# Seven half products for the output of blocks 3 to 8, made transposed from sums of w_out

## The chip, the core and the metric

The kernel runs on one core of a Trainium2 chip. The metric is device time in microseconds (us) of one execution, the median of several runs. A core has five engines that work beside one another and wait for each other by semaphores: TensorE (PE; its weight loads are shown as PEld), VectorE (DVE), ScalarE (ACT), GpSimd (POOL) and SyncE (SP), whose queue here issues nearly all transfers. Every engine executes its own instructions in the order in which they were listed.

## The reference

Attention with 8 batches, 8 heads, 576 positions of 64 dimensions; heads 0 to 3 see the last 32 positions, heads 4 to 7 see positions whose index has the same remainder by 32. Its result, 4608 tokens of 512 numbers, goes through a gated layer of 1536 hidden columns. All of it is in float32.

```python
scores = np.where(masks, scale * q @ k.T, -1e9)          # per batch and head
attn = softmax(scores); x = (attn @ v) laid out as (4608, 512)
gate = 1.0 / (1.0 + np.exp(-(x @ w_gate)))               # (4608, 1536)
val = x @ w_val
out = (gate * val @ w_out).astype(np.float32)            # (4608, 512)
```

## The kernel before

**Precision.** A float32 operand is split into a high part and a rest in the type F32R. Every product is made of three matmuls: high with high, high with low, low with high. So "three" below is always this.

**Tiling.** Tokens are worked on in nine blocks of 512: blocks 0 to 7 are the first 512 positions of each batch, block 8 holds the 64 left-over positions of each. The hidden columns are 12 slices of 128 (f), the 512 input columns are four chunks of 128.

**Blocks 0 to 2** are plain: for each f a gate product (`g`) and a val product (`v`) of 12 matmuls each, ScalarE's sigmoid (`s`), VectorE's product (`m`), the hidden tile's high part by ScalarE (`x`) and low part by VectorE (`y`), then 12 matmuls of the output (`o`: hidden tile stationary, w_out moving, four token tiles of 128 x 512 in two pairs of PSUM banks).

**Blocks 3 to 8** go in three super-blocks of two blocks (k = 3, 5, 7 is the first). Gate and val of two blocks by a pair of slices (q = 0 to 5) are a product of 2 x 2 block matrices, and are made by seven products of half the work in place of eight: `G` (gate) and `V` (val), six matmuls each, for the products p = 1, 2, 6, 5, 7, 4, 3. The moving side are seven sets of sums and differences of x (`xd`, then high parts `xh` by ScalarE and low parts `xl` by VectorE). The stationary side are sums of weights. GpSimd makes them (`pa`, `pb`), ScalarE and VectorE split them (`ph`, `pw`), and they are stored (`pd`; plain ones `pl`) in device memory as `sets`. They come back through a ring of five slots for six sets, 512 KB a set (`r`). PSUM sums of several products are combined by ScalarE's copies (`c`), VectorE's additions (`ad`), ScalarE's sigmoid (`sg`) and VectorE's products (`mu`). The result are the hidden tiles of four quarters: two blocks by two slices.

The output products of blocks 3 to 8 are those of blocks 0 to 2, `o`, 12 matmuls for each block and f: block k's stand between the sets of its own super-block, block k+1's behind them. I call the 42 sets of a super-block its product stage and what follows its output stage.

**Attention** of batches 2 to 7 runs in 24 pieces (n = 0 to 23, four for each block; 12 to 19 are blocks 5 and 6), spread between the products: queries and values are loaded (`LQ`, `LV`), scores (`S`) and values (`X`) are short matmuls, which stand together and which I call an interlude; VectorE has mask, maximum, subtraction, sum, reciprocal, normalization (`M`, `A`, `U`, `N`, `W`) and eight 32-row transposes (`B`), ScalarE the exponential (`E`). The pieces of a super-block have to be done before its sets of x are made.

**Order.** The text `ORDER` lists all steps one by one; each step's instructions are issued to their engines' queues at that place, and no scheduler moves them. SyncE's queue is in the same order: a ring load stands in it behind stores that wait for VectorE and loads that wait for a buffer.

Names of tiles in the rows: `p` and `d` are PSUM accumulators of `G` and `V`, `xs` the sets of x, `ring` a ring slot, `o` (also `o_a`, `o_g`, `o_v`) output accumulators, `hid`, `h`, `e` hidden tiles and what they are made from, `hh`, `hl` the two parts, `sb`, `mx`, `pt` the attention's, `sum`, `sumh` the weight sums.

Of the kernel before, what the change touches and what calls it, by code (L numbers as in the profile page):

```python
# [20 lines left out]
DM, DF = 512, 1536  # L21
# [40 lines left out]
USE = "1265743"  # L62

# [121 lines left out]


@with_exitstack
def attention_then_glu(ctx, tc, qk_l, qk_s, v_l, v_s, w_all, consts, out):
# [11 lines left out]
    def left_over(b):  # L200
# [5 lines left out]
        if b == 6:  # L206
            xr[6] = stage("h0", "xr6").bitcast(F32).rearrange("p (c n) -> p c n", c=NC)
# [423 lines left out]
    def give_out(k, i, cut=slice(0, DM), by=None):  # L631
# [8 lines left out]
        if k < B:  # L640
            return
# [426 lines left out]
```

## Time and profile before

| | |
|---|---|
| runs | 927.53, 928.52, 930.17 us; median 928.52 |
| span of the profiled execution (the page gives it no other time) | 927.6 us |
| TensorE busy | 919.8 us, 99% |
| VectorE busy | 599.9 us, 65% |
| ScalarE busy | 426.8 us, 46% |
| GpSimd busy | 179.9 us, 19% |
| moved by the DMA queues | 154.19 MB, 166 GB/s |

The span runs from the first to the last instruction. An engine's share is a mean over the whole span; stages differ. A row of a group has the line, the engine, the operation, out<-in, the count, the busy time in us, the mean length of one in ns, and the idle time before it. Matmuls are pipelined: the length of one is longer than the distance to the next.

### The profile page before, as it was taken

To read this page: it belongs to the slowest core of one execution; us is meant where nothing else is said; L and a number is where in the kernel's file an instruction comes from. 1 tells how busy PE (TensorE), PEld (TensorE's weight loads), DVE (VectorE), ACT (ScalarE), POOL (GpSimd) and SP (SyncE) were. 2 spreads that over 40 slices of the span, in tenths; PEclk is the share of its full clock that TensorE was granted. 3 is DMA by queue.
4 is the path that set the end of the run, shared out by engine and by line. 5 is a ranking of instruction groups with operands and counts; after the bars stand their busy time and mean duration, and the time that the engine had idled before them with its cause. 6 is when DMAs were issued, how large, how long until landed. Compare 5 with 4: busy or idle time off the path is not lost.

```text
span 927.6 us, 18516 instructions
## 1 busy us (share of the span) xinstructions
PE 919.8 (99%) x7606; PEld 754.9 (81%) x7606; DVE 599.9 (65%) x959; ACT 426.8 (46%) x776; POOL 179.9 (19%) x243
## 2 busy tenths in 40 slices
PE   8999999999999999999999999999999999999998
PEld 5788888888888888888888888888888888888886
DVE  5898877667799899665667896766248333333331
ACT  5888754334546455443435544444335233332222
POOL 4452641554555321000000210000003000000000
PEclk9899999999999999999999999999999999999999
DMA  9862644465677455655645436654443055444111
GB/s 345 333 220 85 197 152 153 159 192 159 199 240 247 115 187 191 208 189 181 193 157 181 149 109 195 198 181 148 138 156 125 23 174 178 145 150 146 59 45 46
DMA packets 90195, 154.19 MB, mean 166 GB/s; under 512 B 5888, under 2 KB 40192, under 8 KB 90112
## 3 DMA queue, kind: packets, MB, share of 16 engines
q1 hardware_dynamic: 89712, 152.36, 50.9%
q8 instruction: 60, 0.98, 0.4%
q10 hardware_dynamic: 400, 0.66, 0.3%
q14 instruction: 23, 0.19, 0.1%
HBM read 121.53 MB, written 31.46 MB: 165 GB/s over the span
## 4 chain that ended last, share of the span: by engine, by line
PE 98%; ACT 1%; DVE 1%; issue 0%; POOL 0%; DVEq 0%; ACTq 0%; POOLq 0%
PE o L623 22%; PE p L887 21%; PE d L887 16%; PE g L592 10%; PE v L592 10%; PE o_a L623 5%; PE o_g L623 3%; PE o_v L623 3%; PE x_a L513 2%; PE x L513 1%; PE s_g L371 1%; PE s_v L371 1%; PE gv L592 1%; PE s L371 1%; PE unread L730 0%; ACT sb L435 0%
## 5 line engine op out<-in xcount | busy, mean ns | idle before, releaser
L887 PE MATMUL p<-xs,ring 128*128 128x512 f32 x864 | 204.6, 389 | 0.0
L887 PEld LDWEIGHTS p<-xs,ring 128*128 128x128 f32 x864 | 162.2, 188 | 33.7
L623 PE MATMUL o<-w,hh 128*128 128x512 f32 x576 | 180.6, 395 | 0.0
L887 PE MATMUL d<-xs,ring 128*128 128x512 f32 x648 | 155.6, 389 | 0.0
L887 PEld LDWEIGHTS d<-xs,ring 128*128 128x128 f32 x648 | 121.6, 188 | 25.2
L623 PEld LDWEIGHTS o<-w,hh 128*128 128x128 f32 x576 | 106.1, 188 | 22.7
L480 DVE STREAM_TRANSPOSE pt<-sb 32x320 f32<-32x320 f32 (+1 forms) x224 | 120.1, 536 | 4.5
L623 PE MATMUL o<-w,hl 128*128 128x512 f32 x288 | 112.0, 389 | 0.0
L921 DVE TENSOR_TENSOR e<-e,d 128x512 f32<-128x512 f32 x54 | 37.1, 687 | 110.6 <-PE d L887 62.5
L592 PE MATMUL g<-xh,w 128*128 128x512 f32 x256 | 85.9, 393 | 0.0
L916 ACT COPY e<-p 128x512 f32<-128x512 f32 x54 | 31.7, 587 | 116.8 <-PE p L887 116.8
L592 PE MATMUL v<-xh,w 128*128 128x512 f32 x256 | 85.2, 390 | 0.0
L623 PEld LDWEIGHTS o<-w,hl 128*128 128x128 f32 x288 | 54.1, 188 | 11.5
L592 PEld LDWEIGHTS g<-xh,w 128*128 128x128 f32 x256 | 48.5, 189 | 10.3
L592 PEld LDWEIGHTS v<-xh,w 128*128 128x128 f32 x256 | 48.0, 188 | 10.0
L815 POOL TENSOR_TENSOR sum<-sum 128x128 f32<-128x128 f32 x96 | 51.5, 540 | 6.3
L592 PE MATMUL g<-xl,w 128*128 128x512 f32 x128 | 50.3, 393 | 0.3 <-DVE xl L553 0.3
L616 DVE TENSOR_TENSOR hl<-hid,hh 128x512 fp32r<-128x512 f32 x36 | 28.0, 780 | 34.5 <-ACT hh L612 34.3
L592 PE MATMUL v<-xl,w 128*128 128x512 f32 x128 | 49.8, 389 | 0.0
L810 POOL TENSOR_TENSOR sum<-w 128x256 f32<-128x256 f32 x44 | 35.5, 827 | 72.7 <-DMA sets<-sum 49.4
L929 ACT ACTIVATE e<-e 128x512 f32<-128x512 f32 x54 | 34.2, 633 | 29.9 <-DVE e L921 29.9
L612 ACT CAST hh<-hid 128x512 fp32r<-128x512 f32 x36 | 22.4, 622 | 49.9 <-PE o_a L623 41.1
(164 smaller groups left out, 1416.6 us busy)
## 6 DMA issues: line engine op xcount, KB each, us to landing
ring<-sets SPq DMA_DIRECT2D x126, 512.0 KB, 4.1
raw<-in_w_all SPq DMA_DIRECT2D x36, 512.0 KB, 5.8
vv<-in_v_l SPq DMA_DIRECT2D x15, 640.0 KB, 4.6
qk<-in_qk_l SPq DMA_DIRECT2D x14, 608.0 KB, 5.2
qk<-in_qk_s SPq DMA_DIRECT2D x14, 594.0 KB, 6.0
out<-ob SPq DMA_DIRECT2D x32, 256.0 KB, 2.0
sets<-w SPq DMA_DIRECT2D x24, 256.0 KB, 3.3
sets<-sumh SPq DMA_DIRECT2D x24, 256.0 KB, 2.8
```

Source lines behind the costliest of these rows:

```text
L371: nc.tensor.matmul(sc[j % len(sc)][g * m : (g + 1) * m, j // len(sc) * BANK + (s - lo) * kk : j // len(sc) * BANK + (s - lo + 1) * kk], q[ ...
L480: nc.vector.transpose(dst[to : to + LB, :, col : col + LB], src[part * LB : (part + 1) * LB, :, h * LB : (h + 1) * LB])
L513: nc.tensor.matmul(at_bank(r, (u * per + g) * m, (u * per + g + 1) * m)[j * D : (j + 1) * D], v[part][rows, slot * P + j * D : slot * P + ...
L592: nc.tensor.matmul(o, w, x, start=first and n == 0, stop=last and n == len(todo) - 1)
L616: by.tensor_tensor(hl, whole_h.pop((k, f)), hh.bitcast(F32), op=ALU.subtract)
L623: nc.tensor.matmul(acc[k][i], h[:, i * P : (i + 1) * P], w, start=f == 0 and n == 0, stop=f == NF - 1 and n == 2,)
L810: nc.gpsimd.tensor_tensor(u[:, at : at + 2], part(wh[f][i], c), part(wl[f][i], c), op=ALU.add)
L815: nc.gpsimd.tensor_tensor(u[:, to], u[:, x], u[:, y], op=op)
L887: nc.tensor.matmul(to, w[:, (wi * 2 + c) * P : (wi * 2 + c + 1) * P], x[xi][:, c], start=p in (1, 2, 5) and c == j == 0, stop=c == 1 and j ...
L916: nc.scalar.copy(x, two[m, 0])
L921: nc.vector.tensor_tensor(x, x, two[m, 1], op=ALU.add)
L929: nc.scalar.activation(x, x, AF.Sigmoid)
```

## The change

The output of a super-block is also made by seven half products. Its result is transposed: 128 columns of the output by 512 tokens, accumulated over all 12 slices. Stationary are w_out's four quarters (by pair of slices and half of the columns) and four sums of them, moving are the hidden tiles and sums of them.

- Sums of w_out: `pa`, `pb`, `ph`, `pw`, `pd` get a third index (i = 2): 12 more of each step, listed from the end of block 2 on through the first product stage; plain quarters are stored by `po` in block 2. They lie in `osets`.
- The ring serves them too: 63 units more, 21 for each super-block behind its 42 sets, one unit for a product and four slices.
- A pair of slices keeps five hidden tiles (`hidden_tile`), in the room that w_out and late weights leave. GpSimd makes the sums in place (`ta`, `tb`, `tc`, `td`).
- An operand is split when its product comes: `hx` (ScalarE, high part), `hy` (VectorE, low part), in five pairs of tiles used in turn. `Oa`, `Ob` are three matmuls each, for the two column tiles. They follow the super-block's 42 sets, product by product, six pairs of slices each.
- Two accumulators for each column tile are used alternately; results are kept by ScalarE (`ok`), added to by VectorE (`oa`) and stored transposed (`os`). A second output holds them; the host only puts the pieces in place.
- The steps from the last third of block 2 on are listed anew. Attention pieces 18 and 19 now stand in the first product stage. Attention matmuls there use the banks that the output accumulators had.

```diff
+HIDDEN = ["w7_0", "w7_1", "w8_0", "w8_1"] + [f"w{f}_2" for f in range(LATE)]
+KEPT = {"1": 0, "2": 1, "6": 0, "5": 4, "7": 2, "4": 1, "3": 3}
+USE_OUT = "1265734"
 ORDER = """
-... G3.5.3 mu3.5.4 x3.11 V3.5.3 ad3.5.0.3 y3.11 sg3.5.3 o3.9 r39 ad3.5.1.3 mu3.5.3 xd5.0.0 X17.0 x4.0 xh5.0.5 y4.0 ...
+... V3.5.3 ad3.5.0.3 sg3.5.3 Oa3.0.1 ad3.5.1.3 r39 xh5.0.3 Oa3.1.1 mu3.5.3 Ob3.0.1 xl5.0.3 ta3.5 Oa3.2.1 hx3.5.1 Ob3.1.1 ...
+    def plain_out_sets(q):
+        to = out_set(q)
+        for n, w in ((0, wh), (1, wl)):
+            a, b = (w[f][2].bitcast(F32).rearrange("p (k c m) -> p k c m", k=2, c=2) for f in (2 * q, 2 * q + 1))
+            nc.sync.dma_start(to[:, 0, n], a[:, 0])
+            nc.sync.dma_start(to[:, 1:3, n], b)
...
-    duos = [(k, q, p) for k in SUPER for q in range(PAIRS) for p in USE]
+    units = []
+    for k in SUPER:
+        units += [(k, q, p) for q in range(PAIRS) for p in USE] + [(k, p, u) for p in USE_OUT for u in range(PAIRS // 2)]
...
+    def hidden_tile(k, q, n):
+        at = 5 * q + n
+        if (k, at // 2) not in hidden:
+            hidden[k, at // 2] = pool.tile([P, 2, TB], F32, tag=HIDDEN[at // 2], name=f"hid{k}_{at // 2}")
+        return hidden[k, at // 2][:, at % 2]
...
+    def out_sum(which):
+        def step(k, q, by=nc.gpsimd):
+            h = [hidden_tile(k, q, n) for n in range(5)]
+            to, x, y = {"a": (4, 2, 0), "b": (2, 3, 2), "c": (0, 3, 4), "d": (1, 1, 0)}[which]
+            by.tensor_tensor(h[to], h[x], h[y], op=ALU.subtract)
...
+    def out_high(k, q, p):
+        u = USE_OUT.index(str(p)) * PAIRS + q
+        if u % 5 < 3:
+            ops[q, p] = [work.tile([P, TB], F32R, tag=f"{n}{u % 5}", name=f"{n}{k}_{q}_{p}") for n in ("hh", "hl")]
+        else:
...
+            ops[q, p] = [op_room[k][:, u % 5 * 2 - 6 + n] for n in range(2)]
+        nc.scalar.copy(ops[q, p][0], hidden_tile(k, q, KEPT[str(p)]))
+
+    def out_low(k, q, p, by=nc.vector):
+        hh, hl = ops[q, p]
+        by.tensor_tensor(hl, hidden_tile(k, q, KEPT[str(p)]), hh.bitcast(F32), op=ALU.subtract)
+
+    def out_half(k, q, p, ms=(0, 1)):
+        w, x = ring[k, str(p), q], ops[q, p]
+        at = int(p in (2, 5, 3))
+        for m in ms:
...
+            for j, (wi, xi) in enumerate(((0, 0), (0, 1), (1, 0))):
+                nc.tensor.matmul(
+                    chains[m, at],
+                    w[:, (wi * 2 + m) * P : (wi * 2 + m + 1) * P],
+                    x[xi],
...
+    def out_store(k, m, p):
+        i, j = {2: (0, 0), 7: (1, 1), 4: (1, 0), 3: (0, 1)}[p]
+        at = (k - SUPER[0] + j) * TB
+        nc.sync.dma_start(out_t[(2 * i + m) * P : (2 * i + m + 1) * P, at : at + TB], out_got[m, {2: 1, 7: 5, 3: 6, 4: 4}[p]])
```

TensorE's instructions at the end of the first product stage, before: `d` is the last set's accumulator, `o` an output step of block 3, `x_a` the values of attention piece 17.

```order
L887 MATMUL d_5_5842<-xs_3_1_4146,ring_5831 128x512
L887 MATMUL d_5_5842<-xs_3_0_4120,ring_5831 128x512
L623 MATMUL o_0_4689<-w_2_1424,hh_9_5688 128x512 x2
L623 MATMUL o_0_4689<-w_2_1424,hl_9_5689 128x512
L623 MATMUL o_0_4689<-w_2_1424,hh_9_5688 128x512 x2
L623 MATMUL o_0_4689<-w_2_1424,hl_9_5689 128x512
L623 MATMUL o_1_4690<-w_2_1424,hh_9_5688 128x512 x2
```

And after: `oc` is an accumulator of the new output products, `hh` and `hl` the operand of a pair of slices.

```order
L930 MATMUL d_5_6056<-xs_3_1_4174,ring_6047 128x512
L930 MATMUL d_5_6056<-xs_3_0_4153,ring_6047 128x512
L1009 MATMUL oc_0_1_6172<-hh_0_1_4686,ring_6074 128x512
L1009 MATMUL oc_0_1_6172<-hl_0_1_4687,ring_6074 128x512
L1009 MATMUL oc_0_1_6172<-hh_0_1_4686,ring_6074 128x512
L1009 MATMUL oc_0_1_6172<-hh_1_1_4923,ring_6074 128x512
L1009 MATMUL oc_0_1_6172<-hl_1_1_4924,ring_6074 128x512
```

The stationary side of the output now comes from the ring, which runs on without a pause; three matmuls belong to one pair of slices, and no output matmul is left inside the product stage.

VectorE's instructions for the third pair of slices in that stage, before: L390 to L459 and L480 are attention, L921 the sums of PSUM accumulators, L938 gate times val, L616 the low part of a hidden tile.

```order
L459 TENSOR_TENSOR sb_2_5033<-sb_2_5033,mx_2_5034 128x640
L480 STREAM_TRANSPOSE pt_2_5072<-sb_2_5033 32x10x32 x2
L921 TENSOR_TENSOR e_2_1_5058<-e_2_1_5058,d_2_5061 128x512
L480 STREAM_TRANSPOSE pt_2_5072<-sb_2_5033 32x10x32 x2
L921 TENSOR_TENSOR h_2_5070<-h_2_5070,d_2_5075 128x512
L480 STREAM_TRANSPOSE pt_2_5072<-sb_2_5033 32x10x32 x4
L938 TENSOR_TENSOR h_2_5070<-h_2_5070,e_2_1_5058 128x512
L616 TENSOR_TENSOR hl_4_5121<-h_2_5070,hh_4_5120 128x512
L921 TENSOR_TENSOR e_2_7_5145<-e_2_7_5145,d_2_5061 128x512
```

And after: L957 and L974 are L921 and L938 of before, L998 is the low part of an output operand, L856 that of a sum of w_out, L430 to L494 and L515 are attention.

```order
L515 STREAM_TRANSPOSE pt_2_5128<-sb_2_5054 32x10x32 x8
L957 TENSOR_TENSOR e_2_1_5123<-e_2_1_5123,d_2_5131 128x512
L957 TENSOR_TENSOR hid_5_5141<-hid_5_5141,d_2_5145 128x512
L856 TENSOR_TENSOR sum_2_1_5057<-sum_2_1_5057,sumh_2_1_5095 128x512
L974 TENSOR_TENSOR hid_5_5141<-hid_5_5141,e_2_1_5123 128x512
L856 TENSOR_TENSOR sum_2_0_5091<-sum_2_0_5091,sumh_2_0_5126 128x512
L998 TENSOR_TENSOR hl_2_1_5228<-hid_5_5141,hh_2_1_5227 128x512
L430 TENSOR_TENSOR sb_3_5180<-s_5230,cst 128x6x54 x2
L446 TENSOR_REDUCE mx_3_5181<-sb_3_5180 128x12
L455 TENSOR_TENSOR sb_3_5180<-sb_3_5180,mx_3_5181 128x12x54
```

A whole second attention piece now begins within the same pair of slices, and the low parts of the sums of w_out stand between the sums of the accumulators and their product.

SyncE's queue at the same place, after: L886 loads a ring set, L864 and L865 store the parts of a sum of w_out, L351 and L338 load the attention's values and queries. Before, ring loads stand there with L316 and L303, the attention's loads, alone.

```order
L864 DMA osets_3272<-sumh_2_0_4948 128x4x128
L865 DMA osets_3272<-sum_2_0_4920 128x4x128
L886 DMA ring_4990<-sets_2554 128x2x512 x2
L351 DMA vv_2_5036<-in_v_l 128x1280
L338 DMA qk_3_5052<-in_qk_s 128x1188
L886 DMA ring_5080<-sets_2554 128x2x512
L886 DMA ring_5107<-sets_2554 128x2x512
```

The stores stand ahead of ring loads in one queue.

## Rows read from the trace of the kernel before

**Rows 1.** The page's first lines: span, and busy us, share and instructions of each engine.

```profile
span 927.6 us, 18516 instructions
PE 919.8 (99%) x7606; PEld 754.9 (81%) x7606; DVE 599.9 (65%) x959; ACT 426.8 (46%) x776; POOL 179.9 (19%) x243
```

**Rows 2.** The page's chain that ended last, by engine.

```profile
PE 98%; ACT 1%; DVE 1%; issue 0%; POOL 0%; DVEq 0%; ACTq 0%; POOLq 0%
```

**Rows 3.** The waits of TensorE: us in total, times, longest.

```profile
PE unread L730 <- POOL ones L725: 1.5, 1, 1.5
PE t L467 <- POOL sb L459: 0.6, 1, 0.6
```

**Rows 4.** The chain in order of time, 376 to 385 us: start, length, what.

```profile
376.64 2.72 PE d L887 x12
379.36 1.36 PE o L623 x6
380.72 1.22 PE x_a L513 x69
...
382.72 1.58 PE o L623 x6
```

**Rows 5.** Three windows: busy (x count) of PE, PEld, DVE, ACT, POOL; PEclk, DMA, GB/s.

```profile
360.30:509.80 149.50, 149.50 (x1222) 123.67 (x1221) 101.77 (x166) 68.88 (x120) 0.73 (x6) 1.00 0.59 186
267.00:296.00 29.00, 29.00 (x358) 23.97 (x354) 27.38 (x45) 16.16 (x33) 16.51 (x27) 1.00 0.72 224
514.30:541.00 26.70, 26.70 (x228) 22.15 (x229) 25.98 (x42) 12.24 (x23) 4.89 (x5) 1.00 0.37 128
```

**Rows 6.** Groups of VectorE by form, 360.3 to 514.3 us: busy, mean ns, idle.

```profile
L480 DVE STREAM_TRANSPOSE pt<-sb 32x384 f32<-32x384 f32 x24 | 13.7, 570 | 0.5
L921 DVE TENSOR_TENSOR e<-e,d 128x512 f32<-128x512 f32 x18 | 12.4, 687 | 13.3 <-ACT e L916 7.8 <-PE d L887 5.3
L480 DVE STREAM_TRANSPOSE pt<-sb 32x320 f32<-32x320 f32 x24 | 12.1, 503 | 0.5
...
L411 DVE TENSOR_REDUCE mx<-sb 128x12 f32<-128x648 f32 x3 | 2.5, 828 | 0.1
...
L395 DVE TENSOR_TENSOR sb<-s_g,cst 128x324 f32<-128x324 f32 x3 | 1.5, 496 | 8.4 <-PE s_g L371 8.4
```

**Rows 7.** Groups of VectorE by form, 141 to 354 us (blocks 1 and 2).

```profile
L616 DVE TENSOR_TENSOR hl<-e,hh 128x512 fp32r<-128x512 f32 x24 | 18.9, 786 | 7.5 <-ACT hh L612 7.0
L824 DVE TENSOR_TENSOR sum<-sum,sumh 128x512 fp32r<-128x512 f32 x24 | 16.8, 722 | 2.1 <-ACT sumh L820 2.0
```

**Rows 8.** Line 616, low parts of hidden tiles: min/median/max ns.

```profile
L616 DVE TENSOR_TENSOR hl<-hid,hh x36: 677/691/1810, 513.0 to 915.7; 128x512 fp32r<-128x512 f32 x36
```

**Rows 9.** Groups of VectorE by form, 703 to 741 us (second output stage).

```profile
L873 DVE TENSOR_TENSOR xs<-xd,xs 128x512 fp32r<-128x512 f32 x8 | 8.8, 1106 | 0.0
...
L861 DVE TENSOR_TENSOR xd<-xraw,xd 128x512 f32<-128x512 f32 x2 | 1.4, 686 | 0.1
```

**Rows 10.** Groups of GpSimd, whole span.

```profile
L815 POOL TENSOR_TENSOR sum<-sum 128x128 f32<-128x128 f32 x96 | 51.5, 540 | 6.3
L810 POOL TENSOR_TENSOR sum<-w 128x256 f32<-128x256 f32 x44 | 35.5, 827 | 72.7 <-DMA sets<-sum 49.4 <-DVE hl L616 11.9 <-DVE mx L451 6.5
...
L861 POOL TENSOR_TENSOR xd<-xraw,xraw 128x512 f32<-128x512 f32 x6 | 9.5, 1576 | 131.2 <-DVE hid L938 126.5 <-ACT sumh L820 2.3 <-ACT xraw L557 1.7
```

**Rows 11.** A group of ScalarE from the page.

```profile
L612 ACT CAST hh<-hid 128x512 fp32r<-128x512 f32 x36 | 22.4, 622 | 49.9 <-PE o_a L623 41.1 <-PE o L623 8.8
```

**Rows 12.** DMA issues on the page: count, KB each, median us to landing.

```profile
ring<-sets SPq DMA_DIRECT2D x126, 512.0 KB, 4.1
...
out<-ob SPq DMA_DIRECT2D x32, 256.0 KB, 2.0
```

**Rows 13.** The page's GB/s in 40 equal slices of the span.

```profile
GB/s 345 333 220 85 197 152 153 159 192 159 199 240 247 115 187 191 208 189 181 193 157 181 149 109 195 198 181 148 138 156 125 23 174 178 145 150 146 59 45 46
```

**Rows 14.** The timeline, 920 to 928 us: the last copy.

```profile
923.47 0.58 ACT L639 COPY ob<-o_a 128x512 f32<-128x512 f32 x1 [1.64 <-PE o_a L623]
```

More of the change, by code (lines that the diff above doesn't have):

```diff
@@ L594, in parts_tiles @@
     def parts_tiles(k, f):
-        hs[k, f] = [work.tile([P, TB], F32R, tag=n, name=f"{n}{k}_{f}", bufs=3) for n in ("hh", "hl")]
+        hs[k, f] = [work.tile([P, TB], F32R, tag=f"{n}{f % 3}", name=f"{n}{k}_{f}") for n in ("hh", "hl")]
         return hs[k, f]
@@ L629, in out_products, with give_out @@
             )
-    def give_out(k, i, cut=slice(0, DM), by=None):
-        tag = ("ost", "l0", "t", "e")[i if k == B else i % 2]
-        if (k, i) not in given:
-            given[k, i] = (odd if tag == "ost" else work).tile([P, DM], F32, tag=tag, name=f"ob{k}_{i}")
-        ob, o = given[k, i], acc[k][i]
-        if by is None:
-            by = (nc.scalar.copy, nc.vector.tensor_copy)[i % 2]
-        by(ob[:, cut], o[:, cut])
-        if k < B:
-            return
-        for n in range(P // REST):
-            at = (i * P // REST + n) * S + TB
-            queue = (nc.scalar, nc.sync)[n if i == NTT - 1 else int(by != nc.scalar.copy)]
-            queue.dma_start(out[at : at + REST, cut], ob[n * REST : (n + 1) * REST, cut])
+    def give_out(k, i):
+        tag = ("ost", "l0")[i % 2]
+        given[k, i] = (odd if tag == "ost" else work).tile([P, DM], F32, tag=tag, name=f"ob{k}_{i}")
+        (nc.scalar.copy, nc.vector.tensor_copy)[i % 2](given[k, i], acc[k][i])
     given = {}
@@ L785, in store @@
     def store(k, i):
[L786 removed]
+        nc.sync.dma_start(out[k * TB + i * P : k * TB + (i + 1) * P], given[k, i])
     sets, sums, sums_h = {}, {}, {}
@@ L804, in plain_sets, with out_set @@
                 nc.sync.dma_start(sets[q][:, 7 * i + 2, n], b[:, 1])
+    out_sets = {}
+    def out_set(q):
+        u = q // 2
+        if u not in out_sets:
+            out_sets[u] = dram.tile([P, 7, 2, 2, 2, P], F32, name=f"osets{u}")
+        return out_sets[u][:, :, q % 2]
+    def plain_out_sets(q):
[4 more added lines that the diff above has]
+            nc.sync.dma_start(to[:, 1:3, n], b)
     def sum_words(q, i, c):
         n = (q * 2 + i) * 2 + c
-        u = sums[q, i, c] = work.tile([P, 4, P], F32, tag=("t", "h0")[n % 2], name=f"sum{q}_{i}_{c}")
-        for at, f in ((0, 2 * q), (2, 2 * q + 1)):
-            nc.gpsimd.tensor_tensor(u[:, at : at + 2], part(wh[f][i], c), part(wl[f][i], c), op=ALU.add)
+        u = sums[q, i, c] = work.tile([P, 4, P], F32, tag=("t" if i < 2 else "h2", "h0")[n % 2], name=f"sum{q}_{i}_{c}")
+        for at, f in ((0, 2 * q), (1, 2 * q + 1)):
+            to = u[:, at::2] if i == 2 else u[:, 2 * at : 2 * at + 2]
+            nc.gpsimd.tensor_tensor(to, part(wh[f][i], c), part(wl[f][i], c), op=ALU.add)
     def sum_parts(*n):
@@ L933, in gate_times @@
         if p == 4:
-            x = work.tile([P, TB], F32, tag="l2", name=f"h{k}_{q}_4")
+            x = hidden_tile(k, q, 1)
             nc.vector.tensor_tensor(x, e, two[1, 0], op=ALU.mult)
```

324 lines of the change are left out of this document (184 added, 140 removed).

## The prediction

> **What bounds the kernel now.** I read the busy shares first: TensorE is busy for 919.8 of the span's 927.6 us, VectorE for 599.9, ScalarE 426.8, GpSimd 179.9 [rows 1]. The chain that ended last is 98% TensorE [rows 2], and the list of waits has next to nothing for TensorE: the longest two are 1.5 and 0.6 us, both at the start [rows 3]. So the time is the sum of what TensorE is given, and everything else is hidden, at present. The chain in order of time gives the price of that work: 12 matmuls of 128x512 take 2.72 us, six take 1.36, whether they are gate/val products or output products [rows 4]. That is 0.2267 us for each. (The 389 ns in the tables of groups is the length of one pipelined matmul and must not be multiplied by a count.) The same rows show one attention interlude, values and scores: 380.72 to 382.72, 2.00 us, and the six matmuls behind it take 1.58 for 1.36, so 2.22 us in all.
>
> What the mean shares hide is VectorE. In the product stage of the first super-block (360.3 to 509.8) it is busy 101.77 of 149.5 us; but in block 2 it is busy 27.38 of 29 us, and after the first product stage 25.98 of 26.7 (97.3%), and TensorE is still busy in all of it [rows 5].
>
> **What the change removes.** Blocks 3 to 8 have 12 slices of hidden columns, 4 token tiles and 3 matmuls each: 6 x 144 = 864 output matmuls. The seven half products need, for each pair of blocks, 7 products x 6 pairs of slices x 2 column tiles x 3 = 252, so 756. 108 matmuls fewer, all of the same 128x512 form, on an engine that never waits: 108 x 0.2267 = 24.5 us. No attention interlude goes or comes. This is the term that I trust most.
>
> **What it adds, and where it lies.** ScalarE: 126 casts to high parts for 72, at 0.622 us [rows 11], 34 us over three super-blocks. An output unit (six matmuls, 1.36 us) needs one such cast and one VectorE subtraction of 0.69 us [rows 8], so both keep up in principle: nothing on the path. GpSimd: 72 sums of hidden tiles at some 1.58 us [rows 10] and 12 sets of weight sums (2 x 0.827 + 4 x 0.540 = 3.81 us each), 160 us in all on an engine that stands idle there; their users come several units later, so nothing by themselves. Transfers: 63 ring loads of 512 KB more and 48 stores of the new sets; a ring load lands in 4.1 us [rows 12], and its slot is freed at least four units, 10.9 us, before its data is wanted. The tail stays: the last copy starts 923.47 [rows 14], 4.1 us before the end of the span; afterwards it is again one ScalarE copy and one store of 256 KB (2.0 us to landing, rows 12). I count it at nothing, at most 0.5 us either way.
>
> **Whom the cover fails.** The product stage of super-block 3 gets shorter and has to hold more of VectorE's work. For TensorE it is 42 sets x 2.72 + 7 interludes x 2.22 = 114.2 + 15.5 = 129.8 us (the same sum for the kernel before, with its nine output steps and five interludes, gives 149.8; the stage took 149.5). For VectorE I go from its 101.77 us [rows 5]: two more attention pieces (18 and 19, which ran beside output products before), each 8 transposes of 0.570 or 0.503, four wide operations near 0.83, two mask additions near 0.49 and a reciprocal, 8.8 us [rows 6]: +17.6. Six low parts of hidden tiles leave the stage: -4.1. Twelve low parts of weight sums come in at 0.722 [rows 7]: +8.7. That is 124.0.
>
> GpSimd now works in that stage too, 67 of 130 us (52%; the weight sums and fifteen sums of hidden tiles). The low part of a hidden tile takes 0.691 as a median but up to 1.810 [rows 8]; in blocks 1 and 2, where GpSimd worked about half of the time (16.51 of 29 in the window of rows 5), its mean was 0.786 [rows 7], 0.1 more. 41 operations of the stage have both inputs in SBUF as that one has: +4.0, so 128.0. VectorE has never been packed more densely than 97.3% [rows 5]; at that it needs 131.6, and TensorE waits 1.8 us. The bounds are 0 (every gap filled, as in block 2 before) and the case of rival B.
>
> In the output stages of super-blocks 3 and 5 the next blocks' sets are made at the same time. Up to the end of the third product (18 units) VectorE has 16 low parts at 0.786, 10 set parts at 1.106 and two differences at 0.686 [rows 9], four sums or products at 0.687 [rows 6], and in super-block 3 the first half of attention piece 20, 2.6: 30.4 us. TensorE has 18 x 1.36 + 2.2 = 26.7. The operands lie in five pairs of tiles, so VectorE may be late by six halves of a unit less the cast and the subtraction: 4.08 - 0.62 - 0.79 = 2.7. The wait is 30.4 - 26.7 - 2.7 = 1.0; in super-block 5, without the attention, 27.8 - 24.5 - 2.7 = 0.6. Later units and super-block 7 have room (37 x 0.69 = 26 of 57 us). Bounds: 0 and some 5.
>
> Sum: 927.6 - 24.5 + 1.8 + 1.0 + 0.6 = 906.5 us for the span. The page gives the profiled execution no time but its span; the median of the three runs is 0.9 above that, and I carry it: 907.4.
>
> **Rivals.** A is the forecast: a gain less short VectorE waits, 905 to 914.
>
> B: VectorE becomes the bound of the first product stage. A low part of 1.810 us is one of 0.691 that stood still for 1.12 us, so a collision may cost half of that, 0.56, on average, whenever GpSimd is at work. With 53 operations of two SBUF inputs there (the weight sums' low parts too) and GpSimd busy 52%: 15.4 us where I took 4.0 and the excess of 0.722; 138.9 us, at 97.3% 142.8, so TensorE waits 13.0 and not 1.8: 919. For it: the change gives GpSimd most of its work in just these stages. Against it: in blocks 1 and 2, with as much GpSimd work, the mean rose by 0.1 only. (The Trainium skill, SBUF — State Buffer, section "SBUF: two separate sides", says that VectorE operations with two SBUF inputs and GpSimd operations take the same port pair under an exclusive lock for a whole instruction, so that the other one stands still. The maxima of rows 8 agree with it; by that rule alone the sum is this rival's.)
>
> C: the new list of steps spaces the work so well that TensorE waits nowhere, as before: 928.5 - 24.5 = 904. For it: no wait in stretches where VectorE is at 94 and 97% [rows 5].
>
> D, on the other side: the ring starves. The first product stage moved 186 GB/s [rows 5]. It now carries 41 ring sets (21.5 MB), 24 stores of weight sums (6.3), seven pairs of attention loads (8.0) and two outputs (0.5): 36.3 MB, 276 GB/s if the stage takes 131.6 us. All of it goes through SyncE's queue in order, where a store that waits for VectorE holds the ring loads behind it. If the stage got no more than block 2's 224 GB/s [rows 5], it would take 162 us, TensorE would wait 32 and the kernel would take 936. It is slower than before from the point where the stage's transfers stay under 36.3 MB / 154 us = 236 GB/s. Against it: slices of the page with 333 and 345 GB/s [rows 13], and a slack of 10.9 us against 4.1.
>
> That the change does not do what it says can be ruled out by the order of its instructions: 756 matmuls write the new accumulators.
>
> **Numbers.** A 0.50, B 0.20, C 0.22, D 0.08. The range runs from C's 904 less 1 for the spread of the runs to just above B, 903 to 920; the likeliest case has 905 to 914. What a measurement of this kernel can tell from no change is about 0.3%, 2.8 us: faster is below 925.7, A, B and C nearly whole, 0.91; within 0.03; slower, D's most part, 0.06.
>
> **What would show it.** TensorE's busy time falls to some 895 us and 12 output matmuls still take 2.72; that is the main step. Waits of TensorE appear in the first product stage, ended by VectorE's sums and products of hidden tiles, and in the first 25 us of the output stages of super-blocks 3 and 5, ended by low parts; none in super-block 7. If instead TensorE waits for transfers, D is right; if low parts and products average over 0.85 us in the first product stage, B is. I am wrong at the root if output matmuls with the weight sums stationary take longer than 0.2267 us, or if the sum of waits passes 12 us.

## The result and the profile after

The changed kernel takes 935.95 us (median of 935.28, 935.69, 936.21, 939.30); the kernel before took 928.35 beside it. The ratio is 1.0088, with a 95% interval of 1.0067 to 1.0109: slower by 0.9%, where 907.4 us was forecast. The profiled execution took 935.28 with a span of 933.5.

The page's first lines, span and busy time of each engine, and its chain that ended last, by engine, after; they answer to [rows 1] and [rows 2].

```profile
span 933.5 us, 18880 instructions
PE 904.4 (97%) x7498; PEld 732.8 (79%) x7498; DVE 675.0 (72%) x1028; ACT 476.4 (51%) x854; POOL 334.1 (36%) x387
...
PE 73%; DVE 14%; DMA 4%; POOL 4%; issue 3%; ACT 2%; SPq 0%; DVEq 0%; POOLq 0%; ACTq 0%
```

108 matmuls are gone, and TensorE's busy time fell by 15.4 us, not by 24.5 (the ends of the pipelined matmuls are modelled, so a part of a wait can count as busy, and two short stretches ran at the lower clock, see the last section). But the chain is no longer TensorE's alone. The waits of TensorE after, us in total, times, longest; before there were two [rows 3]:

```profile
PE oc L1009 <- DVE hl L998: 9.3, 5, 2.8
PE oc L1009 <- DVE ops L998: 2.4, 3, 1.1
PE p L930 <- ACT hid L952: 2.1, 1, 2.1
PE g L627 <- ACT e L635: 2.0, 2, 1.4
PE x L548 <- DVE pt L515: 1.7, 3, 0.7
...
PE x_a L548 <- DVE pt L515: 1.2, 2, 0.7
```

They are three kinds: `oc` in the output stages, `p` and `x` in the first product stage, `g` and `x_a` in blocks 1 and 2. To size them I cut the span at the first matmul of each stage. The next rows are TensorE's instructions on one tile in one stretch: durations, then first and last start. `v<-xh,h` is the val product of a block's last slice, whose weights lie in the tile `h`; its first start, 125.6, is at the end of block 0's products and is my first cut. `p` marks a product stage, `oc` an output stage.

```profile
L627 PE MATMUL v<-xh,h x12: 389/389/389, 125.6 to 353.5; 128*128 128x512 f32 x12
...
L930 PE MATMUL p<-xs,ring x240: 387/389/793, 364.4 to 476.9; 128*128 128x512 f32 x120
L1009 PE MATMUL oc<-hh,ring x104: 387/389/628, 501.6 to 569.5; 128*128 128x512 f32 x104
L930 PE MATMUL p<-xs,ring x168: 388/389/500, 569.7 to 639.0; 128*128 128x512 f32 x168
L1009 PE MATMUL oc<-hh,ring x104: 387/389/402, 691.5 to 757.9; 128*128 128x512 f32 x104
L930 PE MATMUL p<-xs,ring x186: 389/389/389, 758.1 to 830.0; 128*128 128x512 f32 x186
L1009 PE MATMUL oc<-hh,ring x104: 387/389/397, 872.4 to 929.5; 128*128 128x512 f32 x104
```

Against the prediction's prices (2.72 us a set, 1.36 an output unit, 2.22 an interlude):

| stretch | work | took | lost |
|---|---|---|---|
| 125.6 to 364.4 (before: 128.3 to 360.3) | 232.0 | 238.8 | 6.8 |
| product stage 3 | 129.8 | 137.2 | 7.4 |
| output stage 3 | 59.3 | 68.1 | 8.8 |
| product stage 5 (3 interludes) | 120.9 | 121.8 | 0.9 |
| output stage 5 | 57.1 | 66.6 | 9.5 |
| product stage 7, output stage 7 | 114.2, 57.1 | 114.3, 57.5 | 0.5 |

(The work of the first row is what the kernel before took there.)

The losses are 33.9 us where 3.4 were forecast; with a start of the program that was 2.7 us shorter (it differs by as much from run to run), 927.6 - 24.5 - 2.7 + 33.9 = 934.3, the span within 1 us. The main step is right: in the last output stage the chain (start, length, what) shows 252 matmuls without one break, 0.2275 us each (0.2267, and the last one with its whole 0.39).

```profile
872.54 57.33 PE oc L1009 x252
```

So there are three places, each of 7 to 18 us, and each got its experiments.

### The profile page after: what moved, and what is told of

Its sections match the earlier page's. It is cut to its first block, busy times and chain, and to the rows that moved or that the text cites. A ratio compares the mean times of both kernels' runs of the same rounds, so it can differ in the third digit from the quotient of the medians.

```text
span 933.5 us, 18880 instructions
## 1 busy us (share of the span) xinstructions
PE 904.4 (97%) x7498; PEld 732.8 (79%) x7498; DVE 675.0 (72%) x1028; ACT 476.4 (51%) x854; POOL 334.1 (36%) x387
## 4 chain that ended last, share of the span: by engine, by line
PE 73%; DVE 14%; DMA 4%; POOL 4%; issue 3%; ACT 2%; SPq 0%; DVEq 0%; POOLq 0%; ACTq 0%
PE p L930 16%; PE oc L1009 14%; PE d L930 13%; PE o L658 8%; PE v L627 8%; PE g L627 8%; DVE pt L515 3%; POOL sum L847 2%; DVE xs L916 2%; DVE hl L998 2%; DMA sets<-sum 2%; PE x L548 1%; DVE ops L998 1%; POOL sum L842 1%; PE s L406 1%
## 5 line engine op out<-in xcount | busy, mean ns | idle before, releaser
L980 POOL TENSOR_TENSOR hid<-hid,hid 128x512 f32<-128x512 f32 x45 | 64.7, 1438 | 250.8 <-DVE hid L974 250.1
L515 DVE STREAM_TRANSPOSE pt<-sb 32x320 f32<-32x320 f32 (+1 forms) x224 | 120.0, 536 | 4.1
L1009 PE MATMUL oc<-hh,ring 128*128 128x512 f32 x312 | 109.0, 394 | 0.0
L957 DVE TENSOR_TENSOR e<-e,d 128x512 f32<-128x512 f32 x54 | 36.9, 684 | 78.6 <-ACT e L952 40.1
L658 PE MATMUL o<-w,hh 128*128 128x512 f32 x288 | 90.7, 396 | 0.0
L998 DVE TENSOR_TENSOR hl<-hid,hh 128x512 fp32r<-128x512 f32 x78 | 66.4, 861 | 28.8 <-ACT hh L994 28.7
L847 POOL TENSOR_TENSOR sum<-sum 128x128 f32<-128x128 f32 x144 | 81.3, 567 | 10.0
L1009 PE MATMUL oc<-ops,ring 128*128 128x512 f32 x288 | 79.0, 394 | 2.7 <-DVE ops L998 2.4
L1009 PE MATMUL oc<-hl,ring 128*128 128x512 f32 x156 | 62.0, 398 | 9.3 <-DVE hl L998 9.3
L1009 PEld LDWEIGHTS oc<-hh,ring 128*128 128x128 f32 x312 | 59.2, 190 | 12.8 <-ACT hh L994 0.4
L1009 PEld LDWEIGHTS oc<-ops,ring 128*128 128x128 f32 x288 | 53.5, 189 | 17.6 <-DVE ops L998 6.9
L658 PEld LDWEIGHTS o<-w,hh 128*128 128x128 f32 x288 | 52.8, 188 | 11.4
```

Source lines behind the costliest of these rows:

```text
L515: nc.vector.transpose(dst[to : to + LB, :, col : col + LB], src[part * LB : (part + 1) * LB, :, h * LB : (h + 1) * LB])
L658: nc.tensor.matmul(acc[k][i], h[:, i * P : (i + 1) * P], w, start=f == 0 and n == 0, stop=f == NF - 1 and n == 2,)
L847: nc.gpsimd.tensor_tensor(u[:, to], u[:, x], u[:, y], op=op)
L957: nc.vector.tensor_tensor(x, x, two[m, 1], op=ALU.add)
L980: by.tensor_tensor(h[to], h[x], h[y], op=ALU.subtract)
L998: by.tensor_tensor(hl, hidden_tile(k, q, KEPT[str(p)]), hh.bitcast(F32), op=ALU.subtract)
```

## The experiments

I call the stages G3, O3, G5, O5, G7, O7 (product and output stage of super-blocks 3, 5, 7), and "block 2" what lies from 125.6 to G3: blocks 1 and 2, of which only block 2 was listed anew. All lengths below are cut as above, so the start of the program is out of them.

### The output stages

**e2_sums_on_vector.** For super-blocks 3 and 5:

```diff
- tc5.5 ... tb5.5 ... td5.0 td5.1 ...     # GpSimd
+ tcv5.5 ... tbv5.5 ... tdv5.0 tdv5.1 ... # the same subtractions, nc.vector
```

> In the output stages of super-blocks 3 and 5 the nine sums of hidden tiles that GpSimd makes there are made by VectorE at the same places; GpSimd keeps only six differences of x for each. Theory 1 (VectorE lost some 10 us in each of these stages because its operations stand still while GpSimd works on SBUF; 15 GpSimd operations, so 0.65 us for each): VectorE gains 9 x 0.65 = 5.8 us and takes on 9 x 0.69 = 6.2 us, so 934 to 938, and its low parts there average under 0.9 us in place of 1.6. Rival (VectorE simply has too many operations there, whatever GpSimd does): 6.2 us longer in each stage, 946 to 949, with low parts as long as now.

926.62 us, 9.3 less than the changed kernel: O3 64.4, O5 62.3. More work on the engine that was late made both stages some 4 us shorter. The sign rules out plain load; my price of 0.65 us a collision was too low.

**e4_late_differences.** `td5.0` to `td5.5`, and those of super-block 3, taken from between `oa5.0.2` and `hy5.3.5` to behind `hx5.0.7` ... `hx5.4.3`.

> The six GpSimd sums td of the output stages of super-blocks 3 and 5 (the difference that the seventh product wants) are listed behind the fourth product, no longer beside the making of the next sets of x. Theory 1 (collisions of VectorE and GpSimd at 0.65 us for each GpSimd operation): 6 x 0.65 = 3.9 us less wait in each of the two stages, 927 to 930. Rival (plain VectorE load): no VectorE operation is moved, so no change, 935 to 937.

937.60 us, O3 68.9, O5 66.6: no gain. GpSimd's timeline, start and length, has the first of the six, `td3.0` and `td5.0`, first in the changed kernel, then in e4 (whose O3 starts 0.7 and whose O5 1.5 us later):

```profile
518.20 1.73 POOL L980 TENSOR_TENSOR hid<-hid 128x512 f32<-128x512 f32 x1
...
714.47 1.74 POOL L980 TENSOR_TENSOR hid<-hid 128x512 f32<-128x512 f32 x1
```

```profile
528.80 1.74 POOL L973 TENSOR_TENSOR hid<-hid 128x512 f32<-128x512 f32 x1
...
715.95 1.74 POOL L973 TENSOR_TENSOR hid<-hid 128x512 f32<-128x512 f32 x1
```

In O5 nothing moved: GpSimd had nothing else in its queue there, so it started each subtraction when its data was there, as before. In O3 four of the six had stood ahead of two differences of x and started some 10 us later, but still beside low parts: VectorE is busy for 58.08 us of the stage in both runs. So the run took hardly any meeting of the two engines away, and tests neither side.

**e6_stages_without_gpsimd.** e2, and

```diff
-        (nc.vector if n == 1 else nc.gpsimd).tensor_tensor(t, x, y, op=ALU.subtract)
+        (nc.vector if n == 1 or k > SUPER[0] else nc.gpsimd).tensor_tensor(t, x, y, op=ALU.subtract)
```

> As e2, and the six differences of x for each of super-blocks 5 and 7 on VectorE as well: no GpSimd operation is left in the three output stages. Theory 1 (a VectorE operation with two SBUF inputs that meets a GpSimd operation takes 1.7 us for 0.6, so each GpSimd operation costs 1.1 and on VectorE it costs 0.6): 6 x 0.5 = 3 us less than e2 in each of the two stages, 62.1 to 59 us and 64.2 to 61 us, the whole 919 to 922, no low part of an output operand over 0.9 us there. Rival (VectorE is now simply full, its own differences delay its low parts): no gain on e2, 925 to 928.

922.18 us: O3 61.9, O5 59.4, 6.1 and 7.3 us less than the changed kernel; VectorE has 15 operations more in each. Groups by form in O5: the changed kernel (691.5 to 758), and then e6 (its O5, 687.7 to 747.1). Count, busy time, mean ns:

```profile
L998 DVE TENSOR_TENSOR hl<-hid,hh 128x512 fp32r<-128x512 f32 x23 | 20.8, 919 | 7.0 <-ACT hh L994 7.0
L998 DVE TENSOR_TENSOR ops<-hid,ops 128x512 fp32r<-128x512 f32 x14 | 13.8, 999 | 3.6 <-ACT ops L994 3.5
L916 DVE TENSOR_TENSOR xs<-xd,xs 128x512 fp32r<-128x512 f32 x8 | 8.5, 1077 | 0.0
L1025 DVE TENSOR_TENSOR ot<-ot,oc 128x512 f32<-128x512 f32 x6 | 4.1, 678 | 0.0
```

```profile
L991 DVE TENSOR_TENSOR hl<-hid,hh 128x512 fp32r<-128x512 f32 x23 | 15.7, 692 | 7.0 <-ACT hh L987 7.0
L991 DVE TENSOR_TENSOR ops<-hid,ops 128x512 fp32r<-128x512 f32 x14 | 9.7, 692 | 2.4 <-ACT ops L987 2.3
L909 DVE TENSOR_TENSOR xs<-xd,xs 128x512 fp32r<-128x512 f32 x8 | 5.5, 688 | 0.0
```

With GpSimd gone every low part is back at 0.69 us. `ot<-ot,oc`, which reads one operand from PSUM, had been 0.68 all along.

**e10_idle_work.** The price by itself, where no sets are made:

```diff
+    def idle_work(k):
+        t = pool.tile([P, 2, TB], F32, tag="w0_0", name="idle")
+        for _ in range(30):
+            nc.gpsimd.tensor_tensor(t[:, 0], hidden_tile(k, 0, 2), hidden_tile(k, 0, 3), op=ALU.subtract)
```

> Added: 30 GpSimd subtractions of 128x512 in SBUF, of hidden tiles into a tile that nobody reads, listed in the output stage of super-block 7, where GpSimd is otherwise idle and no sets are made. Theory 1 (a VectorE operation with two SBUF inputs and a GpSimd operation exclude each other, so that beside GpSimd working without a pause VectorE ends one operation in 1.7 us, where TensorE uses one in 1.36): the low parts there average over 1.3 us in place of 0.69, and TensorE waits (30 x (1.70 - 1.36)) - 2.7 = 7.5 us, stage 57.1 to some 64 us; VectorE's additions from PSUM stay at 0.67. Rival (VectorE was late in the other stages because of its number of operations): low parts under 0.9 us, stage 57 to 58 us.

948.16 us (one execution): O7 takes 70.9 for 57.5. VectorE's timeline while GpSimd works without a pause (start, length, xcount), and GpSimd's row for all of it:

```profile
879.99 50.63 POOL L982 TENSOR_TENSOR idle<-hid 128x512 f32<-128x512 f32 x30
930.58 1.26 POOL L973 TENSOR_TENSOR hid<-hid,hid 128x512 f32<-128x512 f32 x1
931.80 1.27 POOL L973 TENSOR_TENSOR hid<-hid 128x512 f32<-128x512 f32 x1
```

```profile
912.77 3.47 DVE L996 TENSOR_TENSOR ops<-hid,ops 128x512 fp32r<-128x512 f32 x2
916.17 5.18 DVE L996 TENSOR_TENSOR hl<-hid,hh 128x512 fp32r<-128x512 f32 x3
921.27 0.67 DVE L1023 TENSOR_TENSOR ot<-ot,oc 128x512 f32<-128x512 f32 x1
921.87 1.18 DVE L996 TENSOR_TENSOR ops<-hid,ops 128x512 fp32r<-128x512 f32 x1
```

Without GpSimd, in e6's O5, the next operation starts 0.60 us behind a low part:

```profile
692.33 0.69 DVE L991 TENSOR_TENSOR hl<-hid,hh 128x512 fp32r<-128x512 f32 x1
692.93 0.69 DVE L973 TENSOR_TENSOR hid<-hid 128x512 f32<-128x512 f32 x1
```

The two take turns: 50.63 / 30 = 1.69 us for one GpSimd operation, and VectorE ends one low part in the same 1.70 us (from start to start 3.40 us for two, 5.10 for three). GpSimd alone, while VectorE had nothing to do at 930.6, needed 1.22 from start to start. So a pair takes 1.69, nearly the sum of both alone (0.60 + 1.22 = 1.82). The addition from PSUM runs inside GpSimd's turn, in 0.67; the low part behind it ends 1.70 us after the low part before it (at 921.35 and 923.05).

13.4 us were lost where 7.5 were forecast. TensorE's timeline has 3.9 of them as waits at 932.5 and 933.7 (3.25 and 0.62), a consequence that I had not seen: the operands of the seventh product, `td`, stood in GpSimd's queue behind the added work. Some 1.7 more are the clock's. It was granted at 0.50 (1.2 GHz of 2.4) from 933.51 to 936.92, right behind these waits (the window's clock stands behind POOL's count), and the chain's last 32 matmuls took 9.07 us, where 32 x 0.2267 and the last one's end give 7.4. The remaining 0.3 I can't place.

```profile
932.54 0.50 PE L1007 MATMUL oc<-hh,ring 128*128 128x512 f32 x1 [3.25 <-ACT hh L992]
933.67 0.80 PE L1007 MATMUL oc<-hl,ring 128*128 128x512 f32 x1 [0.62 <-DVE hl L996]
```

```profile
933.51:936.92 3.41, 3.25 (x8) 2.58 (x9) 3.27 (x5) 1.28 (x3) 3.41 (x3) 0.50 0.04 16
```

```profile
933.67 9.07 PE oc L1007 x32
```

### Block 2

**e1_po_spread.** `po0` to `po5` listed behind `g2.6` to `g2.11`, one each.

> The six stores of plain w_out quarters stand one each behind the gate products of slices 6 to 11 of block 2, not in one run behind slices 1 to 3. Theory 1 (that run of stores keeps the DMA engines full at 342 GB/s, so a GpSimd weight sum waits 17 us for the landing of the store that frees its room, ScalarE's in-order cast waits for GpSimd, and the sigmoids behind it keep TensorE waiting): block 2 gets its 7 us back, the whole takes 928 to 931. Rival (the waits come from the attention and weight steps of block 2 themselves, listed more densely than before): 934 to 937, with the same waits in 240 to 300 us.

935.89 us. Block 2 gained 1.8 us (237.1), G3 lost 2.1 (139.3). In 260 to 280 us the chip moved 164 GB/s in place of 345, so the run of stores was dissolved; it was not the main cause.

**e5_block2_as_before.** The steps from `E4`, just ahead of block 2's first product `g2.0`, to `G3.0.1` in the order of before, `po` as in e1, `pa0.2.0 pb0.2.0` at the end.

> The last third of block 2 is listed as it was before (the same steps; the quarter stores one each behind the gate products of slices 6 to 11, the first weight sum at the end), all behind it as in the changed kernel. Theory 1 (the new order of the same steps in block 2 costs 7 us: VectorE has the attention steps, the splits and the differences in an order in which it waits for GpSimd and ScalarE): the first product stage starts some 6 us earlier, the whole takes 928 to 931. Rival (it is the added stores and sums that slow block 2, whatever the order): 934 to 937.

930.04 us; block 2 takes 233.5, 5.3 less. Two windows of the changed kernel, and of e5 (busy of PE, PEld, DVE, ACT, POOL, then PEclk, DMA share, GB/s):

```profile
240.00:300.00 60.00, 58.51 (x706) 47.42 (x705) 52.69 (x87) 31.35 (x59) 29.71 (x47) 1.00 0.89 289
300.00:364.40 64.40, 61.17 (x717) 49.36 (x715) 55.42 (x89) 30.75 (x59) 21.67 (x30) 1.00 0.49 155
```

```profile
240.00:300.00 60.00, 58.94 (x710) 48.27 (x709) 54.85 (x90) 32.47 (x60) 28.92 (x48) 1.00 0.70 212
300.00:358.80 58.80, 58.80 (x711) 48.49 (x710) 54.10 (x87) 30.51 (x58) 18.17 (x24) 1.00 0.76 243
```

Behind 300 us TensorE has no break at all, with VectorE at 54.10 of 58.80 us. The steps are the same but for the first sum of w_out, which now stands at the end, and two steps of attention piece 12 (`E12`, `D12`), which stand ahead of G3 as before. So it is their order; less e1's part, it is worth 3.5 us. Which of the exchanged steps does it, that first sum included, was not tried.

### The first product stage

**e3_third_room.** A third tile for the sums of w_out:

```diff
-tag=("t" if i < 2 else "h2", "h0")[n % 2]
+tag=("t", "h0")[n % 2] if i < 2 else ("h2", "h0", "l2")[(2 * q + c) % 3]
```

> The sums of w_out use three rooms in turn and not two, so GpSimd waits for the store before the last but one. Theory 1 (in the first product stage GpSimd's wait for the landing of the stores, 16.6 us in four waits, makes ScalarE and so TensorE wait): TensorE's wait there falls from 7.4 to about 4 us, the whole to 932 to 934. Rival (TensorE's waits there come from VectorE, full and slowed by GpSimd, and the stores are beside it): no change, 935 to 937.

942.01 us, G3 144.8. The edit was not what I had meant: in the order in which the sums are listed it gives the tiles 0 1 0 2 2 1 1 0 0 2 1 2, three times the same one to two neighbours, and GpSimd's waits for a landing grew from 16.6 to 27.8 us.

**e7_third_room_in_turn.** The index is a count of the sums made.

> As e3 was meant to be: three rooms for the sums of w_out, used strictly in turn (in e3 two sums that follow each other often had the same room, and the first product stage took 144.8 us for 137.2). Theory 1 (in that stage the weight sums are a chain: GpSimd waits for a store's landing to get its room, ScalarE waits in order for GpSimd's sum, and copies for TensorE stand behind it): GpSimd's wait for landings falls from 16.6 us to under 5, the stage from 137.2 to some 134, the whole to 931 to 934. Rival (TensorE's waits there come from VectorE): stage 136 to 139, the whole 934 to 937.

937.72 us, G3 137.4: the rival, though GpSimd's waits for a landing fell from 16.6 to 5.8 us.

**e9_late_casts.** e7, and `ph`, `pw`, `pd` of each sum listed behind the next sum's `pb`.

> Three rooms in turn as in e7, and the cast, low part and stores of each sum of w_out are listed behind GpSimd's next sum, not behind their own. Theory 1 (in the first product stage ScalarE waits in order for GpSimd's sums, 17.9 us in nine waits, and the copies of TensorE's banks stand behind these casts): ScalarE's wait for GpSimd falls under 5 us, the stage from 137.2 to 131 to 133 us, the whole to 930 to 932 (a start of the program that differs by up to 3 us from run to run aside). Rival (GpSimd's sums slow VectorE by collisions, wherever the casts stand): stage 136 to 138.

937.61 us, G3 139.6. Two of ScalarE's waits in G3, of the changed kernel and then of e9: for GpSimd's sums, and for VectorE's additions.

```profile
ACT sumh L852 <- POOL sum L847: 17.9, 9, 3.7
ACT e L965 <- DVE e L957: 14.3, 8, 3.8
```

```profile
ACT e L960 <- DVE e L952: 27.5, 10, 6.0
...
ACT sumh L847 <- POOL sum L842: 0.4, 1, 0.4
```

ScalarE's longest wait of the stage was taken away and the stage did not get shorter. My theory fell: ScalarE then waited for VectorE instead. (The edit moves VectorE's low parts of the sums too, so it is not a clean test of ScalarE alone.)

**e8_no_sums_of_w_out**, **e11_no_low_parts**, **e12_fill_for_sums** leave out parts of the sums:

```diff
+                nc.sync.dma_start(to[:, 3:5, n], a)   # e8: pa, pb, ph, pw, pd of i = 2 not listed,
+                nc.sync.dma_start(to[:, 5:7, n], b)   #     po spread as in e1
...
+        if n[1] == 2: return                          # e11: in sum_low
...
+            nc.gpsimd.memset(u, 0)                    # e12: for the six operations of pa, pb
```

> Left out: the twelve sums of w_out and their splits (GpSimd, ScalarE and VectorE have 72, 12 and 12 operations less); in their places of the sets plain quarters of w_out are stored in block 2, with the quarter stores, which stand behind the gate products of slices 6 to 11. Ring loads and matmuls are as many as before. Theory 1 (the weight sums as a whole, their chain and their collisions with VectorE, cause the first product stage's loss of 7.4 us): that stage takes 130 to 132 us in place of 137.2, the whole 927 to 930. Rival (the two more attention pieces fill VectorE, weight sums or not): stage 135 to 138, the whole 932 to 936.

> Left out: the twelve low parts of the sums of w_out on VectorE (their place in the sets gets the sums themselves); GpSimd's sums, ScalarE's casts and the stores stay. Theory 1 (GpSimd's 72 operations slow VectorE by collisions, or hold up ScalarE): the first product stage gains little, 134 to 137 us. Rival (VectorE has too many operations in that stage, and these twelve are what is too much): 130 to 132 us, like e8's 130.4.

> Left out: the arithmetic of the twelve sums of w_out on GpSimd, in whose place one fill of the tile with zeros stands (12 operations for 72); casts, low parts and stores stay. Theory 1 (GpSimd's work beside VectorE is the cause): the first product stage takes 130 to 133 us in place of 137.2. Rival (VectorE's own low parts of the sums are the cause): 135 to 138 us.

932.26, 931.31 and 931.12 us. G3 takes 130.4, 133.0 and 133.4 (e8's block 2 took 241.4, with twice the stores, and its start 2.2 us longer; so its gain shows in the whole only in part). Windows over all of G3, of the changed kernel, e8, e11 and e12:

```profile
364.40:501.60 137.20, 132.64 (x1357) 107.85 (x1356) 122.50 (x199) 78.65 (x140) 64.75 (x89) 0.99 0.83 265
```

```profile
369.10:499.50 130.40, 129.87 (x1357) 106.91 (x1356) 112.50 (x187) 72.27 (x128) 21.90 (x23) 1.00 0.71 232
```

```profile
366.40:499.40 133.00, 130.69 (x1358) 106.74 (x1357) 113.31 (x187) 77.91 (x140) 62.19 (x89) 1.00 0.84 274
```

```profile
364.20:497.60 133.40, 131.07 (x1358) 106.85 (x1357) 119.97 (x199) 78.36 (x140) 27.77 (x34) 1.00 0.84 273
```

e8: without the weight sums 6.8 of the 7.4 us are gone. What the two more attention pieces would give back with the sums kept was not tried, so the loss is of both together, and the sums are enough to take it away. e11: VectorE's low parts alone (9.2 us of VectorE) are worth 4.2. e12: GpSimd's arithmetic is worth 3.8, though VectorE's time falls by 2.5 only, so there its collisions are few. Both expectations were half right: e11 lies between theory and rival, e12 just outside theory 1. Whether e12's part beyond the 2.5 us is ScalarE's wait stays open, since e9 took that wait away by another way without a gain.

**v3_g3_on_vector**: v2 (below), and `ta`, `tb`, `tc` of `3.0` to `3.4` on VectorE.

> As v2 (block 2 in the order of before, no GpSimd operation in the output stages), and the fifteen sums of hidden tiles of the first product stage on VectorE too; GpSimd has only the sums of w_out there. Theory 1 (collisions: 1.1 us for each GpSimd operation that VectorE meets, 0.6 on VectorE): that stage falls from 137.5 to 131 to 134 us, the whole to 910 to 914. Rival (VectorE is full there by its number of operations): stage 138 to 145, the whole 917 to 924.

920.36 us, G3 142.3, VectorE busy 129.97 of it: the rival. Its window over G3:

```profile
357.90:500.20 142.30, 133.89 (x1357) 108.26 (x1356) 129.97 (x215) 76.94 (x138) 47.48 (x80) 0.99 0.79 256
```

Here 15 operations more cost 4.8 us, where in O3 and O5 they gave back 6 to 7. The same exchange has opposite signs in two stages of one kernel. What differs is how much the meetings took: in G3 VectorE's busy time rose by 6.8 us over v2's 123.19, where fifteen operations of 0.69 are 10.4, so only some 3.6 us of meetings went; in O5 the three groups shown under e6 alone fell from 43.1 to 30.9 us.

### A version that beats both

**v2_order_and_vector** is e5 and e6, **v1_all** e5, e6 and e9.

> e5 and e6 together: block 2 in the order of before, no GpSimd operation in the output stages. If both causes are separate, their gains add: 935.5 - 5.6 - 12.5 = 917 us, 916 to 920. If what block 2 gives back is lost in the first product stage (its weight sums start as late as now), 921 to 923.

> e5, e6 and e9 together. If the three causes add: 917 less the 5 us of e9, 911 to 914 us. If e9's theory is wrong, as v2: 916 to 920.

v2 takes 916.54 us, 0.9888 [0.9873, 0.9903] of before; the gains of e5 and e6 add. v1 takes 919.06 (0.9917 [0.9900, 0.9933]), its G3 141.5: e9's listing costs there. v2's G3 still takes 137.5, its O3 61.9 and its O5 59.3; the span of its profiled execution is 915.0 us.

## Why the prediction was wrong

**The removed matmuls**, -24.5 us, were right: 252 in 57.33 us. So were super-block 7 and the tail: next to no loss (0.5). By the prediction's own sign, a sum of waits over 12 us, the rest of it was wrong at the root.

**The wait in output stages 3 and 5**, +1.0 and +0.6, is the term that failed most: 8.8 and 9.5. I counted the operations rightly. What failed is the length of the low parts, 0.786: I took it from blocks 1 and 2 [rows 7]. The 16 low parts of the first three products measured 1.26 in O3 and 1.29 in O5 as a mean, single ones between 0.68 and 1.78; that alone is 7.6 and 8.0 us. The set parts, 1.106 from the output stage before [rows 9], measured 1.11 in O5. In that stage GpSimd had made only differences of x; after the change it makes nine sums more there, and beside GpSimd working without a pause a low part takes 1.70 (e10). I had put the sums at "nothing by themselves", because their users come late; their cost lay on VectorE, not on their users. Of the two losses, 18.3 us together, 13.4 went with GpSimd (e6), although VectorE took on 15 operations in each stage; of the 4.9 left, 2.9 are TensorE's waits for low parts, so VectorE's load.

This is rival B's mechanism in another stage. The Trainium skill, SBUF — State Buffer, section "SBUF: two separate sides", has the rule beside that rival, which I gave 0.20: VectorE with two SBUF inputs and GpSimd hold one port pair for a whole instruction. e10 nearly agrees: 1.69 us for a pair against 1.82 for both alone. I argued against it with a mean of blocks 1 and 2, +0.1 us; but there GpSimd's operations are 0.54 and 0.83 long [rows 10], those of the change 1.7 in O5, and a mean over a stage says nothing of a stretch of 25 us in which both have work without a pause.

**The first product stage**, +1.8: 7.4. The sum of VectorE's work was too high, not too low (128.0 forecast, 122.50 measured). Collisions were priced a little low: 4.0, where e12 and v3 give some 2.5 and 3.6. B's own sign, low parts and products over 0.85 us in this stage, was not there: the low parts of hidden tiles took 0.69, the products 0.74, only the low parts of the sums 0.86. What failed was "VectorE has never been packed more densely than 97.3%; at that it needs 131.6". It was 89% packed when TensorE waited. So it needed room well before it was full: taking 9.2 us of VectorE away gave TensorE 4.2 back (e11), adding 6.8 cost 4.8 (v3's 129.97 against v2's 123.19). The reason that I give is argued, not shown by a run: VectorE works in order and its load comes in bursts, as an interlude wants a whole attention piece by a given set. (The chain from 435 to 450 us in G3 is mostly VectorE's steps of one attention piece, and TensorE's `x` behind them.)

**Block 2** had no term: 6.8. The prediction put it at nothing without a reason. That its steps stand in another order, and this from the first slice of the block on and not from its last third as I described it, I left out, though VectorE was busy for 27.38 of 29 us in it [rows 5]. e5 got 5.3 of the 6.8 back.

Rival D named the right time, 936 (its own terms add up to 937.8: 906.5 - 1.8 + 32.2 + 0.9), by luck and for a wrong reason: TensorE waited for no ring load, and G3 moved 265 GB/s, well over the 236 at which D would have decided.

## What to carry to other kernels

An operation moved to an idle GpSimd was not free here: where VectorE is busy with operations on two SBUF inputs beside it, price each meeting at nearly the sum of both lengths, and give the work to VectorE if that is the less. The same exchange lost where they met less (v3), so price it stage by stage. Where an engine that works in order is as busy as VectorE was here (86 to 92% in the stretches that lost or regained time), a new order of the same steps can have a price; forecast it by stage, and count the waits on that engine rather than its sum of work. And before an experiment moves a step in the list, look whether anything in its queue or its data holds it at the old time.

## What was not expected of the hardware

In G3 the granted clock fell once. The window's clock (behind POOL's count) and a piece of the chain in it:

```profile
440.00:460.00 20.00, 18.87 (x186) 15.34 (x185) 18.88 (x32) 12.51 (x19) 8.58 (x15) 0.91 0.89 273
```

```profile
451.80 4.38 PE p L930 x12
456.17 2.72 PE d L930 x12
```

Twelve matmuls took 4.38 us for 2.72, part of them at 1.2 GHz (the clock was granted at 0.5 from 451.39 to 454.81). Before it TensorE had waited 2.13 of the 20 us from 420 to 440, and from 448 on had only short matmuls with waits between them. But these 1.66 us did not make the stage longer. e5 and v2 list G3 alike, step by step; in e5 the clock fell there too, in v2 it did not, and both take 137.5 us. First e5, then v2:

```profile
358.80:496.30 137.50, 133.41 (x1357) 107.87 (x1356) 123.38 (x200) 77.33 (x138) 68.94 (x95) 0.99 0.82 265
```

```profile
358.80:496.30 137.50, 132.22 (x1358) 106.77 (x1357) 123.19 (x200) 76.89 (x138) 68.64 (x95) 1.00 0.82 265
```

The same holds for O3: in the changed kernel the clock fell from 533.31 to 536.73, behind a wait of 2.8 us, in e10 it did not fall there, and O3 takes 68.1 in both. In these stages TensorE would have waited for VectorE anyway, and the lower clock cost nothing; at the end of e10's O7, where nothing was left to wait for, it cost some 1.7 us.

e10's rows also show GpSimd's 128x512 subtraction at 1.22 us from start to start when VectorE is still, for 1.69 when it is not: GpSimd loses in the meetings too.
